# Load order, zero fills, root, softmax place and last stores of a one-core attention and GEGLU kernel

**The chip, the cores and the metric.** One core of one Trainium2 chip. Times are device microseconds (us) of one execution; the profile shows another, recorded one, with its own time. Engines in the profile: PE is TensorE's matmul side, PEld its weight load, DVE is VectorE, ACT ScalarE, POOL GpSimd; SP issues the transfers, and SPq and the like are an engine's queue.

## The reference

A layer norm without weights, a sliding dilated attention of 32 heads of width 16 (8 keys, every second position back) and a GEGLU block side by side, and the sum of both with the input:

```python
def _layernorm(x, axis=-1, eps=1e-5):
    return (x - mean) / jnp.sqrt(var + eps)          # cut: mean and var over the last axis

def _A_ref(x, wqkv, wo):                              # H = 32, Dh = 16, W = 8, dil = 2
    q, k, v = ...                                     # x @ wqkv, split by head
    kg = k[:, :, idx_c, :].reshape(B, H, S, W, Dh)    # idx = pos - 2 * arange(8)
    logits = jnp.einsum("bhsd,bhswd->bhsw", q, kg) * scale
    logits = jnp.where(mask[None, None, :, :], logits, -1e9)
    attn = _softmax(logits, axis=-1)
    o = jnp.einsum("bhsw,bhswd->bhsd", attn, vg)
    return o.reshape(B, S, D) @ wo                    # cut: a transpose

def _B_ref(x, w_gate, w_up, w_down):
    return (gelu(x @ w_gate) * (x @ w_up)) @ w_down   # Dff = 1376

xn = _layernorm(x)                                    # x: 1 x 2048 x 512, bf16
return x + _A_ref(xn, A_wqkv, A_wo) + _B_ref(xn, B_w_gate, B_w_up, B_w_down)
```

## The kernel before

The kernel states its work as tasks. Each has an engine, a name, an assumed duration, what it reads and writes, and a priority. A list scheduler in the file turns them into one fixed order per engine and sets the semaphores. So an edit of a priority can move many instructions. The parts that the change touches, in outline (some lines are shortened, and those with a bare task name stand for the whole task):

```python
SHIFT = {"acc0": 555, "acc1": 267, ...}               # cut: priority offsets by group
SCHED = dict(PE_SLACK=1.0, DMA_BPUS=250e3,
             TOL=dict(pe=1.0, act=-0.3, dve=0.3, pool=-0.3, sp=0.0))
# ... zero fills on GpSimd: the dummy matmuls' source, and a padding row block of Wd and of HT
G.task("pool", "c_wsrc", 0.8, lambda e: e.memset(wsrc[:, :], 0.0), wr=[I_wsrc], prio=PC - 1)
G.task("pool", "c_wdz", 0.3, lambda e: e.memset(Wd[0:32, 10, :], 0.0), wr=[(I_wd, 2)], prio=PC2 + 20)
G.task("pool", "c_htz", 0.3, lambda e: e.memset(HT[0:32, :, 10, :], 0.0), wr=[I_htz], prio=PC2 + 20)
# ... loads, all on one queue: Wq, Wk, Wv at -900, -899, -898; x0 in two halves at -960;
#     x1 (row tiles 2 and 3 in one load) at -899.5, so the queue has x0 x0 Wq x1 Wk
t_ld["w" + nm] = G.task("sp", "ld_w" + nm, 0, mk(), wr=[(I_wq, nm)], prio=-900 + i, nbytes=512 * 1024)
# ... layer norm of row tile t: statistics, aggregate, variance + eps, root by GpSimd's power,
#     reciprocal, subtraction, scaling; then four PE transposes
"bnst%d"  # dve bn_stats          "bnag%d"  # dve bn_aggr        "ve%d"    # dve add 1e-5
"sq%d"    # pool pow 0.5          "rstd%d"  # dve reciprocal     "sub%d"   # dve (tile 0: act)
"norm%d"  # dve scaling           "tpx.."   # pe transposes      "evx.."   # act eviction
chain(["bnst0", "bnag0", "ve0", "bnst1", "rstd0", "norm0", "bnag1", "ve1", "sub1", "rstd1", "norm1",
       "bnst2", "bnag2", "ve2", "sub2", "bnst3", "rstd2", "norm2", "bnag3", "ve3", "sub3", "rstd3",
       "norm3"])                                      # dve order of tiles 0 to 3
# ... the softmax of one block of 512 rows: logits in two PSUM banks (lgv), the rest in SBUF (DE)
"d1_%d"   # dve max over the 8 keys, from PSUM
"d2_%d"   # dve DE = logits - max
"exp%d"   # act DE = exp(DE)
"d4_%d"   # dve strided sum of DE      "d5_%d"  # dve reciprocal      "d6_%d"  # dve PB = DE * that
# ... the last matmuls (4 with Wo, 11 with Wd), the last add and the last stores
TAIL_SPLIT = [14, 15]                                 # the last two row tiles in two parts of 256
```

At the start PE first runs dummy matmuls on zeros (tile wsrc). Then it transposes the four tiles of block 0 one by one, and between them makes the q and k projections of each. The fixed order of PE is: transposes 0, q projection of tile 0, transposes 1, k of 0, q of 1, transposes 2, k of 1, transposes 3, and on.

## Time and profile before

| | before |
|---|---|
| median of 3 runs (range) | 197.95 us (197.94 to 198.12) |
| time of the profiled run, its span | 198.39 us, 196.6 us |
| PE busy | 188.7 us, 96% of the span |
| start of the last of the four transposes | 12.70 us |
| from there to the end of PE's last matmul | 181.39 us |
| from there to the last store's landing | 2.10 us |

In a timeline line the first number is the start in us from the span's start, the second the length, then engine, source line, operation, tiles, and in brackets the idle time of the engine just before it and what ended it. One more passage of the timeline belongs to those that the prediction shows; it is why the fourth tile (index 3) came late:

```profile
9.08 0.94 POOL L824 MEMSET HT<- 32x1024 bf16 x1
...
11.08 0.70 DVE L920 BATCH_NORM_STATS2 st<-XIN 128x6 f32<-128x512 bf16 x1 [0.38 <-DMA XIN<-in_A_x_dram]
...
11.91 0.13 DVE L943 RECIPROCAL rstd<-sq 128x1 f32<-128x1 bf16 x1
...
12.29 0.35 DVE L967 TENSOR_SCALAR XIN<-XIN,rstd 128x512 bf16<-128x512 bf16 x1
```

The statistics at 11.08 are those of row tile 4, which nobody needs yet. They stand in VectorE's list ahead of tile 3's reciprocal (11.91) and scaling (12.29), which PE waits for.

### The profile page before, as it was taken

How to read it: one execution, taken by the hardware profiler on the slowest of the kernel's cores; microseconds unless marked ns; L12 is line 12 of the kernel's file. 1: busy time of each engine (PE TensorE's matmuls, PEld its weight loads, DVE VectorE, ACT ScalarE, POOL GpSimd, SP SyncE). 2: the span in 40 equal slices, each digit the busy share in tenths (PEclk: the TensorE clock that was granted, in tenths of full speed). 3: DMA queues.
4: the chain of work that ended last, by engine and by line, in shares of the span. 5: the costliest groups of instructions: out<-in, count | busy, mean ns of one | idle time of the engine just before them, and what ended most of it. 6: DMA issues, size and time to landing. Idle time of an engine off the chain costs nothing.

```text
span 196.6 us, 3169 instructions
## 1 busy us (share of the span) xinstructions
PE 188.7 (96%) x1189; PEld 90.6 (46%) x1208; DVE 153.6 (78%) x238; ACT 103.6 (53%) x167; POOL 21.4 (11%) x37
## 2 busy tenths in 40 slices
PE   7689999999999999999999999999999999999994
PEld 2486444444444443444444444444444443444483
DVE  3788999999999399998999889988791897142131
ACT  4366673687787758701647930473894105766000
POOL 6834001020870100000000000000000000000000
PEclk9999999999999999999999999999999999999999
DMA  5999999894444678054538036248414260010121
GB/s 127 363 370 332 318 175 147 227 279 94 106 126 110 179 121 210 0 145 125 161 107 213 5 118 171 64 129 210 114 53 110 71 169 27 0 34 25 36 84 42
DMA packets 34639, 27.03 MB, mean 137 GB/s; under 512 B 10976, under 2 KB 33088, under 8 KB 34624
## 3 DMA queue, kind: packets, MB, share of 16 engines
q1 hardware_dynamic: 34624, 26.83, 52.9%
q8 instruction: 9, 0.15, 0.3%
q14 instruction: 6, 0.05, 0.1%
HBM read 19.99 MB, written 5.26 MB: 128 GB/s over the span
## 4 chain that ended last, share of the span: by engine, by line
PE 91%; DMA 4%; SPq 1%; DVE 1%; issue 1%; ACT 0%; DVEq 0%
PE PS L1326 35%; PE PS L1405 19%; PE PS L1084 18%; PE PS L1401 7%; PE PS L1168 4%; DMA XIN<-in_A_x_dram 4%; PE PS L1295 3%; PE PS L1040 2%; PE PS L1361 2%; PE PS L1161 1%; SPq L859 1%; SPq L905 0%; DVE st L920 0%; ACT UU L1343 0%; SPq L909 0%
## 5 line engine op out<-in xcount | busy, mean ns | idle before, releaser
L1405 PE MATMUL PS<-Wd,HT 128*128 128x512 bf16 (+1 forms) x197 | 41.3, 355 | 0.1
L1326 PE MATMUL PS<-xnT,Wu 128*128 128x512 bf16 x158 | 40.2, 379 | 0.1
L1326 PE MATMUL PS<-xnT,Wg 128*128 128x512 bf16 x153 | 39.6, 379 | 0.7 <-issue 0.3
L1274 DVE TENSOR_TENSOR UNI<-BS,PT 128x2048 bf16<-128x2048 bf16 x32 | 37.2, 1219 | 2.2 <-PE PS L1295 2.1
L1138 DVE TENSOR_TENSOR UNI<-QT,KT 128x2048 bf16<-128x2048 bf16 x32 | 37.3, 1216 | 0.9 <-ACT KT L1059 0.9
L1336 ACT ACTIVATE GG<-PS 128x512 bf16<-128x512 f32 x40 | 24.0, 600 | 23.7 <-PE PS L1326 23.7
L1084 PE MATMUL PS<-xnT,Wqkv 128*128 128x512 bf16 x157 | 35.9, 379 | 0.3 <-issue 0.2
L1343 ACT ACTIVATE UU<-PS 128x512 bf16<-128x512 f32 x40 | 23.9, 601 | 7.7 <-PE PS L1326 7.7
L1405 PEld LDWEIGHTS PS<-Wd,HT 128*128 128x128 bf16 x198 | 19.4, 98 | 18.7
L1348 DVE TENSOR_TENSOR HT<-GG,UU 128x512 bf16<-128x512 bf16 x40 | 15.8, 415 | 12.4 <-ACT UU L1343 11.8
L1326 PEld LDWEIGHTS PS<-xnT,Wg 128*128 128x128 bf16 x160 | 15.3, 98 | 19.8 <-ACT UU L1343 0.8
L1326 PEld LDWEIGHTS PS<-xnT,Wu 128*128 128x128 bf16 x160 | 15.5, 98 | 19.2 <-ACT GG L1336 0.4
L1084 PEld LDWEIGHTS PS<-xnT,Wqkv 128*128 128x128 bf16 x160 | 15.4, 98 | 18.8 <-issue 0.4
L1425 DVE TENSOR_TENSOR OB<-PS,XR 128x512 bf16<-128x512 f32 (+1 forms) x18 | 11.3, 630 | 15.5 <-PE PS L1405 15.4
L1108 ACT ACTIVATE VT<-PS 128x512 bf16<-128x512 f32 x16 | 9.5, 596 | 13.7 <-PE PS L1084 13.7
L1401 PE MATMUL PS<-Wo,OT 128*128 128x512 bf16 (+1 forms) x67 | 16.2, 354 | 0.2
L1306 ACT ACTIVATE OT<-PS 128x512 bf16<-128x512 f32 x16 | 8.7, 595 | 13.2 <-PE PS L1295 13.2
L920 DVE BATCH_NORM_STATS2 st<-XIN 128x6 f32<-128x512 bf16 x16 | 10.8, 685 | 3.8 <-DMA XIN<-in_A_x_dram 3.8
L937 POOL TENSOR_TENSOR sq<-ve,mhalf 128x2 bf16<-128x2 f32 (+1 forms) x10 | 6.6, 662 | 34.7 <-DVE ve L931 34.7
L1401 PEld LDWEIGHTS PS<-Wo,OT 128*128 128x128 bf16 x72 | 7.1, 98 | 7.0
L1124 POOL COPY KT<-KT 128x64 bf16<-128x64 bf16 x3 | 9.4, 3118 | 7.7 <-ACT KT L1101 6.0
L1094 ACT ACTIVATE QT<-PS 128x512 bf16<-128x512 f32 x12 | 7.1, 595 | 4.8 <-PE PS L1084 4.8
(62 smaller groups left out, 142.8 us busy)
## 6 DMA issues: line engine op xcount, KB each, us to landing
BS<-vt_scratch SPq DMA_DIRECT2D x64, 128.5 KB, 3.0
vt_scratch<-VT SPq DMA_DIRECT2D x16, 128.0 KB
XR<-in_A_x_dram SPq DMA_DIRECT2D x16, 128.0 KB, 2.1
XIN<-in_A_x_dram SPq DMA_DIRECT2D x7, 256.0 KB, 7.2
out_dram<-OB SPq DMA_DIRECT2D x14, 128.0 KB, 1.9
Wqkv<-in_A_wqkv_dram SPq DMA_DIRECT2D x3, 512.0 KB, 6.6
Wg<-in_B_w_gate_dram SPq DMA_DIRECT2D x1, 1280.0 KB
Wu<-in_B_w_up_dram SPq DMA_DIRECT2D x1, 1280.0 KB
```

The source lines that it names most:

```text
L920: return lambda e: e.bn_stats(out=st[:, t, :], in_=XIN[:, it.slot, t2, :])
L1084: ins = e.matmul(PS[:, 512 * it.slot:512 * it.slot + HWD], lhsT=lhsT, rhs=xnT[:, itx.slot, kt, c0:c0 + HWD], start=(kt == 0), stop=(kt == 3))
L1108: return lambda e: e.activation(out=VT[:, ito.slot, 0:HWD], in_=PS[:, 512 * it.slot:512 * it.slot + HWD], func=ACTF.Identity)
L1138: return lambda e: e.tensor_tensor(out=UNI[:, it.slot, :, :], in0=bass.AP(QT, (itq.slot * 4 + g) * 512, [[NQT * 4 * 512, 128], [0, 4], [1, ...
L1274: return lambda e: e.tensor_tensor(out=bass.AP(UNI, ito.slot * 2048, [[NUNI * 2048, 128], [512, 4], [128, 4], [1, 128]]), in0=bass.AP(BS, ...
L1326: ins = e.matmul(PS[0:M, 512 * it.slot:512 * it.slot + 512], lhsT=Wx[:, kt, j * 128:j * 128 + M], rhs=xnT[:, itx.slot, kt, :], start=(kt = ...
L1336: return lambda e: e.activation(out=GG[0:M, ito.slot, :], in_=PS[0:M, 512 * it.slot:512 * it.slot + 512], func=ACTF.Gelu_apprx_tanh)
L1343: return lambda e: e.activation(out=UU[0:M, ito.slot, :], in_=PS[0:M, 512 * it.slot:512 * it.slot + 512], func=ACTF.Identity)
L1348: return lambda e: e.tensor_tensor(out=HT[0:M, ito.slot, j, :], in0=GG[0:M, ig.slot, :], in1=UU[0:M, iu.slot, :], op=ALU.mult)
L1401: ins = e.matmul(PS[:, 512 * it.slot:512 * it.slot + CW], lhsT=OT[:, ito.slot, dq, ti * 128:(ti + 1) * 128], rhs=Wo[:, dq, c0:c1], start=( ...
L1405: ins = e.matmul(PS[:, 512 * it.slot:512 * it.slot + CW], lhsT=HT[:, ith.slot, j, ti * 128:(ti + 1) * 128], rhs=Wd[:, j, c0:c1], start=Fal ...
L1425: return lambda e: e.tensor_tensor(out=OB[:, ito.slot, 0:CW], in0=PS[:, 512 * it.slot:512 * it.slot + CW], in1=XR[:, itx.slot, c0:c1], op= ...
```

## The change

The intent: bring both weight blocks of the first projections ahead of x1, keep GpSimd out of VectorE's way, get the first two tiles' roots sooner, take a slow strided sum out of SBUF, and leave less to do after the last matmul. The core of the diff (cut: the removal of DE's helpers, the `it_pb` lines, items that are only declared, a part that is switched off; the NMS and NSUBA lines gather settings that stand one by one in the file: the N.. are numbers of buffers, NSUBA and NSQA the numbers of row tiles whose subtraction and whose root ScalarE does):

```diff
-SHIFT = {"acc0": 555, "acc1": 267, ...}
+SHIFT = {"acc0": 47, "acc1": -436, ...}               # cut: all offsets set anew
-SCHED = dict(PE_SLACK=1.0, ... TOL=dict(pe=1.0, act=-0.3, dve=0.3, ...))
+SCHED = dict(PE_SLACK=1.6, ... TOL=dict(pe=0.6, act=-0.3, dve=-0.3, ...))
-    NMS 2, NDE 1, NBS 3, NOB 2, NSUBA 1
+    NMS 1, NBS 4, NOB 3, NSUBA 0, NSQA 2
-    TAIL_SPLIT = cfg.get("TAIL_SPLIT", [14, 15])
+    TAIL_SPLIT = {14: [(0, 256), (256, 512)], 15: [(0, 256), (256, 384), (384, 512)]}
-        G.task("pool", "c_wsrc", 0.8, ... prio=PC - 1)
+        G.task("dve", "c_wsrc", 0.25, ... prio=PC - 1)
-        G.task("pool", "c_wdz", 0.3, ... prio=PC2 + 20)
-        G.task("pool", "c_htz", 0.3, ... prio=PC2 + 20)
+        G.task("dve", "c_wdz", 0.25, ... prio=PC + 1)
+        G.task("dve", "c_htz", 0.4, ... prio=PC + 2)
-            out=onef[:, 1:2], in_=onef[:, 0:1], func=ACTF.Gelu_apprx_tanh),
+            out=onef[:, 1:2], in_=onef[:, 0:1], func=ACTF.Sqrt),
-            ... prio=-900 + i, nbytes=512 * 1024)                     # Wq, Wk, Wv
+            ... prio=(-958, -957.5, -898)[i], nbytes=512 * 1024)
-                prio=(0, -899.5, -897.5, -897)[p] ...                 # x1 and later
+                prio=(0, -957, -897.5, -897)[p] ...
+                def mk_sa(t=t):
+                    return lambda e: e.activation(out=sq[:, t:t + 1], in_=mv[:, t, 1:2], func=ACTF.Sqrt,
+                                                  bias=eps[:, 0:1])
+                if t < NSQA:
+                    t_of["sq%d" % t] = G.task("act", "sq%d" % t, 0.15, mk_sa(), ...)
-        chain(["bnst0", "bnag0", "ve0", "bnst1", "rstd0", "norm0", "bnag1", "ve1", "sub1", ...
-               ... "norm3"])
+        chain(["bnst0", "bnag0", "sub0", "rstd0", "norm0", "bnst1", "bnag1", "sub1", ...
+               ... "norm3", "bnst4"])
+        chain(["norm3", "bnst5"])
+        chain(["evx0_0", "sq1"])
-                    out=dev(), in0=lgv(...), in1=msb(0), op=ALU.subtract)
+                    out=lgv(...), in0=lgv(...), in1=msb(0), op=ALU.subtract)
-                return lambda e: e.activation(out=DE[...], in_=DE[...], func=ACTF.Exp)
+                return lambda e: e.activation(out=lgv(...), in_=lgv(...), func=ACTF.Exp)
-                return lambda e: e.tensor_reduce(out=msv(1), in_=devw(), axis=AX.X, op=ALU.add)
+                return lambda e: e.tensor_reduce(
+                    out=msv(1), in_=lgv(0, 128, [(1, 128), (128, 8)]), axis=AX.X, op=ALU.add)
-                    in0=dev(), in1=msb(2), op=ALU.mult)
+                    in0=lgv(0, 128, [(512, 2), (128, 4), (1, 128)]), in1=msb(2), op=ALU.mult)
```

## The prediction

> **What bounds the kernel now.** I read the page's busy table first, then its picture of 40 slices, then the list of who waited for whom on TensorE, then the timeline of the two stretches that these leave: the first 13 us and the last 10 us.
>
> ```profile
> PE 188.7 (96%) x1189; PEld 90.6 (46%) x1208; DVE 153.6 (78%) x238; ACT 103.6 (53%) x167; POOL 21.4 (11%) x37
> ...
> PE   7689999999999999999999999999999999999994
> ```
>
> TensorE (PE) is busy 188.7 of 196.6 us, and its row dips only in the first three slices and the last one; slice four to slice 39 are full. Because a busy PE is not proof of a dense PE, I checked the spacing: in the list of the chain in order of time, 40 matmuls of 512 columns (the projection, from 44.21) take 8.63 us, 0.2157 us each, and the same 0.216 holds wherever I looked. The work itself cannot be packed more tightly, and no part of the change takes a matmul away.
>
> ```profile
> engine line waited for: us in total, times, longest us
> PE PS L1040 <- DMA Wqkv<-in_A_wqkv_dram: 1.6, 2, 0.9
> PE PS L850 <- POOL wsrc L800: 1.4, 1, 1.4
> PE PS L992 <- DVE XIN L967: 0.7, 1, 0.7
> PE PS L1326 <- issue: 0.3, 2, 0.2
> PE PS L992 <- DVE XIN L964: 0.2, 1, 0.2
> ```
>
> Every wait of PE above 0.3 us belongs to the head: two for the q and k weights (L1040), one for the zeros of the dummy matmuls (L850), two for normalized rows that it transposes (L992). After the last transpose all waits together are about 0.7 us. So the middle, some 167 us, has almost nothing to give; only head and tail do.
>
> ```profile
> 2.98 0.69 DVE L920 BATCH_NORM_STATS2 st<-XIN 128x6 f32<-128x512 bf16 x1 [2.98 <-DMA XIN<-in_A_x_dram]
> ...
> 4.16 0.57 POOL L937 TENSOR_TENSOR sq<-ve,mhalf 128x1 bf16<-128x1 f32 x1 [0.95 <-DVE ve L931]
> ...
> 6.73 1.05 PE L1040 MATMUL PS<-xnT,Wqkv 128*128 128x128 bf16 x16 [0.66 <-DMA Wqkv<-in_A_wqkv_dram]
> ...
> 7.36 0.69 DVE L920 BATCH_NORM_STATS2 st<-XIN 128x6 f32<-128x512 bf16 x1 [0.41 <-DMA XIN<-in_A_x_dram]
> ...
> 8.90 1.96 PE L1040 MATMUL PS<-xnT,Wqkv 128*128 128x128 bf16 x32 [0.90 <-DMA Wqkv<-in_A_wqkv_dram]
> ...
> 9.42 0.75 DVE L967 TENSOR_SCALAR XIN<-XIN,rstd 128x512 bf16<-128x512 bf16 x1
> ...
> 12.70 0.40 PE L992 MATMUL PS<-ident,XIN 128*128 128x128 bf16 x4 [0.72 <-DVE XIN L967]
> ```
>
> This is the head: x rows 0 and 1 land by 3.4; Wq ends the wait at 6.7; the third and fourth row tile (one load, x1) at 7.36; Wk at 8.9; the fourth tile is normalized at 12.64 and its transpose starts at 12.70. From there PE never stops, so the head is worth what moves this 12.70.
>
> **What the Trainium skill says.** "DMA: Bandwidth & Descriptors", Queues, rings and completion order: on each DMA engine the descriptors of one issuing sequencer are consumed in ring order. The trace agrees: Wq, x1, Wk land in the order of their issues, about 0.7 us for x1's 256 KB and 1.5 us for Wk's 512 KB, some 350 GB/s. So moving Wk ahead of x1 is an exchange, not a gain. "SBUF — State Buffer", SBUF: two separate sides, says VectorE in a two-port mode and GpSimd exclude each other; the trace agrees, for the scaling at 9.42 took 0.75 us beside GpSimd's memset of HT (9.08 to 10.02) and 0.35 elsewhere. "VectorE: DVE Perf Modes", the perf-mode tier table: a reduce and an fp32 tensor_tensor run at the base rate, in SBUF or PSUM. For the tensor_tensor the trace agrees, 1.22 us from PSUM and 1.21 from SBUF; for the reduce it does not quite:
>
> ```profile
> L1224 DVE TENSOR_REDUCE ms<-DE 128x128 f32<-128x1024 f32 x4 | 7.7, 1914 | 2.1 <-ACT DE L1219 2.1
> ...
> L1208 DVE TENSOR_REDUCE ms<-PS 128x128 f32<-128x1024 f32 x4 | 4.9, 1221 | 0.6 <-PE PS L1168 0.6
> ```
>
> The same strided sum costs 1.91 us from SBUF and 1.22 from PSUM. "ScalarE: Activation LUTs", What ACT_TABLE_LOAD costs: a table load is 1283 ns, as in this trace (1.28), and one more is needed, since the first table is now the root's and the GELU's is loaded later.
>
> **The change part by part.** *First loads.* The queue now has x0, x0, Wq, Wk, x1. Wq keeps its third place, so the first projection still starts near 6.7. Wk comes when 256 KB less lies ahead of it: 8.85 - 0.74, about 8.1. x1 comes where Wk came: 8.85 instead of 7.33.
>
> *Root on ScalarE, zero fills on VectorE.* For the first two tiles the variance's add (0.15) and GpSimd's power (0.57 to 0.60, with hand-overs 0.85) become one ScalarE activation of one column. The ScalarE subtraction at 3.92 took 0.72 for 512 columns; its slope leaves about 0.3 for one column. The first tile's transpose can start near 4.9 instead of 5.46. The dummy matmuls start near 1.1 instead of 1.38, as VectorE fills their source at 0.8 with nothing before it. None of this reaches the path: the next thing, the q projection, waits for Wq at 6.6 anyway. Worth 0. The two other fills leave GpSimd, so the 0.75 us scaling becomes 0.35; that does count, for it is in the chain of tile three.
>
> *The new chain to the last transpose.* VectorE's order is now fixed: all of tiles two and three before tile four, where before the statistics of tile four cut in at 11.08 and held the reciprocal to 11.91. I lay it out with start-to-start gaps from the trace. Statistics at 8.88; aggregate +0.73; add +0.21; subtract +0.07; next statistics +0.26 (10.15); reciprocal +0.61; scaling +0.18 (10.94); next aggregate +0.27; add +0.20; GpSimd power +0.24 and 0.59 long; reciprocal at 12.27; scaling 12.47 to 12.82; transpose at 12.87. The chain from landing to transpose shrinks from 5.34 to 4.0 us, the landing comes 1.52 later, and the sum is 12.87 against 12.70: **+0.17 us**. PE's earlier start on the k projection (8.1 for 8.9) ends in a longer wait before tile two's transpose, near 10.1 to 11.3.
>
> *Softmax in PSUM.* The strided sum saves 0.69 us four times on VectorE; the subtraction, exponential and scaling stay at 1.22, 1.06 and 1.21. It lies beside matmuls, so it is worth 0 directly. Its price is that a pair of the eight PSUM banks is held until the scaling, not until the subtraction. By the order of instructions, the first pair is wanted again 12 groups of matmuls after it was filled (12 x 0.863 = 10.4 us), the next two over 20 us after; the softmax of block 0, with other VectorE work between, comes to about 9 us by the durations above. Enough, with some 1.4 us of slack.
>
> *The new order in the middle.* PE does the same groups in another order. Products, exponentials and GELUs stay ahead of their matmuls when I sum durations along both orders, with 1 us or so of slack at the tightest places. I count back 0.1 of the present waits: **-0.1**.
>
> *Tail.*
>
> ```profile
> 192.81 1.25 PE L1405 MATMUL PS<-Wd,HT 128*128 128x256 bf16 x10
> ...
> 194.18 0.42 DVE L1425 TENSOR_TENSOR OB<-PS,XR 128x256 bf16<-128x256 f32 x1 [1.18 <-PE PS L1405]
> ```
>
> The last 15 matmuls of 256 columns (1.64 us in the chain) become 30 of 128. The q projection shows 48 such in 2.68 us, 0.056 each, so 30 take 1.68: +0.04. The last add goes from 0.42 to about 0.29, by the step from 0.69 at 512 columns to 0.42 at 256: -0.13. The last store is 32 KB instead of 64; the issue list gives 1.5 us for 64 KB and 1.9 for 128 KB, so perhaps -0.1, less if short rows are poor.
>
> Sum: 0.17 - 0.1 + 0.04 - 0.13 - 0.1 = -0.12 us, from 197.95 to 197.83. I predict **197.8 us**.
>
> **Rivals.** *The weight wait was the bound and is gone.* For it: the 0.9 us wait at 8.9 is the largest after the start. If tiles two and three were ready in time, PE would go from 8.1 without a stop and the head would give 0.8 to 1.0: 197.0. Against it: x1 pays for it in ring order. It would need x1 to land well before 8.85, for instance because the slow start of the transfers (97 GB/s between 3 and 4 us, by the table of stages) is not repeated.
> *PSUM becomes the bound.* A held pair makes PE wait for the scaling four times, 0.5 to 1 us each: 199 to 201. For it: VectorE is 99% busy from 20 to 64 us, so a late product or a late sum passes on. Against it: the saved 0.69 us and the bank distances above.
> *The added table load stalls PE.* 1.28 us on ScalarE near 20 us, when GELU starts: with several banks free, hidden; if not, +0.5.
> *PE stays the bound and nothing shows.* That is my case: within half a microsecond of before.
>
> **Range and chances.** Head and tail together can hardly give more than 1.2 us, and 2% is 3.96 us, half of all the time in which PE does no real work (5.5 us before the first transpose, 2.5 after the last matmul, and little else). So faster by over 2% is nearly excluded. Slower by over 2% needs a repeated PSUM stall. The range 196.8 to 198.8 holds the weight rival at one end and one or two stalls at the other. Chances: faster 0.01, within 2% 0.97, slower 0.02.
>
> **What would show it.** Right: in the timeline the projection starts near 6.7 again; tile two's statistics start near 8.9; PE's waits show VectorE's scaling before the transposes, some 1.2 and 0.3 us, in place of the second weight wait; the last transpose starts near 12.9; the reduce shows 1.22 us; no PE wait over 0.3 us after 14; the last add takes 0.29. Wrong: x1 landing before 8.3, the weights before 6.2, or a PE wait for the softmax's scaling.

## The result and the profile after

The changed kernel took 197.90 us in the median of 4 runs (197.67 to 198.14), the kernel before 198.03 in 4 runs beside it (197.94 to 198.28). The ratio is 0.9991, interval 0.9974 to 1.0009: the same. Ratios here and below are the mean time of one kernel's fast runs over that of the other's of the same rounds, so not quite the ratio of the medians that are quoted.

The page after, busy table and PE's row of the picture:

```profile
PE 190.6 (97%) x1223; PEld 91.1 (46%) x1223; DVE 153.8 (79%) x241; ACT 104.0 (53%) x169; POOL 9.6 (5%) x33
...
PE   7879999999999999999999999999999999999995
```

PE's row is full from slice four to 39 as before. GpSimd went from 21.4 to 9.6 us. PE's 190.6 against 188.7 is no added work to speak of: 15 matmuls became 30 of half the width, and no matmul records are missing (1,223 for 1,223 weight loads; before 1,189 for 1,208). The waits of PE after, all that are listed:

```profile
PE PS L1026 <- DVE XIN L1001: 1.4, 2, 1.1
PE PS L864 <- DVE wsrc L813: 1.2, 1, 1.2
PE PS L1076 <- ACT xnT L1037: 0.3, 1, 0.3
```

The two waits for weights (1.6 us) are gone in this trace, and the two waits for normalized rows have grown from 0.9 to 1.4 us (the longer one 1.1). The timeline of the head after:

```profile
6.39 1.07 PE L1076 MATMUL PS<-xnT,Wqkv 128*128 128x128 bf16 x16 [0.26 <-ACT xnT L1037]
...
7.51 1.95 PE L1076 MATMUL PS<-xnT,Wqkv 128*128 128x128 bf16 x32
...
8.13 0.69 DVE L945 BATCH_NORM_STATS2 st<-XIN 128x6 f32<-128x512 bf16 x1 [1.04 <-DMA XIN<-in_A_x_dram]
...
10.61 0.40 PE L1026 MATMUL PS<-ident,XIN 128*128 128x128 bf16 x4 [1.14 <-DVE XIN L1001]
...
12.15 0.40 PE L1026 MATMUL PS<-ident,XIN 128*128 128x128 bf16 x4 [0.26 <-DVE XIN L1001]
```

The k projection (7.51) no longer waits. VectorE waits for x1 until 8.13, and PE waits 1.14 us for tile 2. The last transpose starts at 12.15, against 12.70, and it seems that 0.55 us was won here. Most of that is not the change: the first loads are held up in the fourth microsecond, and when they land differs from run to run. The trace's table of DMA shows it for the kernel before; first the stretch from 3 to 4 us, then the one from 5 to 6:

```profile
DMA packets 98, 0.10 MB, mean 97 GB/s; under 512 B 3, under 2 KB 98, under 8 KB 98
```

```profile
DMA packets 395, 0.38 MB, mean 381 GB/s; under 512 B 23, under 2 KB 395, under 8 KB 395
```

From 3 to 4 us the queue moved a quarter of what it moved two microseconds later. In all ten traces it is slow there: 85 to 158 GB/s, after 219 to 254 in the microsecond before, and 351 to 388 from 5 to 6. The profiled run of the kernel before had drawn a poor start: it took 198.39 us, 0.36 above the median of the rounds, and its Wq, the third load in every one of these kernels, landed at 6.59, the latest of the ten traces (5.67 to 6.59). So the landing of Wq is the yardstick of a run's draw, and the table of all traces gives the last transpose less that landing too. This takes it that what stands behind Wq in the queue does not move its landing: it came at 5.95 to 6.59 with x1 behind it and at 5.67 to 6.48 with Wk, ranges that overlap; more is not shown. Landings are the last of a load's 16 parts in the trace's records.

| trace | Wq | Wk | x1 | last transpose | less Wq | last transpose to PE's end |
|---|---|---|---|---|---|---|
| before | 6.59 | 8.85 | 7.33 | 12.70 | 6.11 | 181.39 |
| after | 6.03 | 7.44 | 8.11 | 12.15 | 6.12 | 181.41 |
| x1 first again (e1) | 5.95 | 8.07 | 6.61 | 11.03 | 5.08 | 181.41 |
| VectorE's order only (e2) | 6.13 | 8.57 | 6.81 | 11.53 | 5.40 | 181.38 |
| tail undone (e3) | 6.04 | 7.43 | 8.11 | 12.15 | 6.11 | 181.37 |
| sum twice (e4) | 5.67 | 7.20 | 7.88 | 11.92 | 6.25 | 181.44 |
| load order only (e5) | 5.83 | 7.31 | 8.06 | 12.96 | 7.13 | 181.39 |
| root on GpSimd (e6) | 6.35 | 7.73 | 8.40 | 12.42 | 6.07 | 181.41 |
| x1 split (e7) | 6.20 | 8.01 | 8.36 (second half) | 11.13 | 4.93 | 181.42 |
| after, once more (e8) | 6.48 | 7.87 | 8.61 | 12.66 | 6.18 | 181.41 |

Read by that yardstick, before (6.11, one trace) and after (6.12, 6.18) have the same head within 0.07 us. And the last column is the same in ten traces to 0.07 us: in both orders of the middle, once PE has its last transpose, it needs 181.4 us.

Two further groups after, from the list by line and shape (busy us and mean ns after the bar), are the strided sum and the GELU's table loads:

```profile
L1367 ACT ACT_TABLE_LOAD x5 | 6.4, 1283 | 0.1
...
L1254 DVE TENSOR_REDUCE ms<-PS 128x128 f32<-128x1024 f32 x4 | 4.9, 1225 | 1.7 <-ACT PS L1249 1.4
```

The sum now takes 1,225 ns for 1,914, and there are five GELU loads for four. The end of the timeline after:

```profile
193.65 0.29 DVE L1456 TENSOR_TENSOR OB<-PS,XR 128x128 bf16<-128x128 f32 x1 [0.55 <-PE PS L1436]
```

The last add takes 0.29 us for 0.42. From PE's end to the last store's landing it is 1.88 us (193.56 to 195.44), against 2.10 before (194.09 to 196.19).

### The profile page after: what moved, and what is told of

Same layout as the page of the kernel before. It is cut to its first block, busy times and chain, and to the rows that moved or that the text cites. A ratio compares the mean times of both kernels' runs of the same rounds, so it can differ in the third digit from the quotient of the medians.

```text
span 196.0 us, 3243 instructions
## 1 busy us (share of the span) xinstructions
PE 190.6 (97%) x1223; PEld 91.1 (46%) x1223; DVE 153.8 (79%) x241; ACT 104.0 (53%) x169; POOL 9.6 (5%) x33
## 4 chain that ended last, share of the span: by engine, by line
PE 93%; DMA 3%; DVE 2%; SPq 1%; issue 0%; POOL 0%; DVEq 0%
PE PS L1357 36%; PE PS L1436 19%; PE PS L1120 18%; PE PS L1432 7%; PE PS L1326 4%; PE PS L1204 4%; DMA XIN<-in_A_x_dram 3%; PE PS L1076 2%; PE PS L1392 2%; PE PS L1197 1%; DVE st L945 1%; SPq L881 0%; SPq L929 0%; DVE XIN L1001 0%; POOL sq L969 0%
## 5 line engine op out<-in xcount | busy, mean ns | idle before, releaser
L1436 PE MATMUL PS<-Wd,HT 128*128 128x512 bf16 (+2 forms) x209 | 41.3, 345 | 0.0
L1357 PE MATMUL PS<-xnT,Wg 128*128 128x512 bf16 x160 | 40.3, 379 | 0.0
L1374 ACT ACTIVATE UU<-PS 128x512 bf16<-128x512 f32 x40 | 24.0, 600 | 10.5 <-PE PS L1357 10.4
L1456 DVE TENSOR_TENSOR OB<-PS,XR 128x512 bf16<-128x512 f32 (+2 forms) x19 | 11.5, 605 | 17.7 <-PE PS L1436 17.7
L1432 PE MATMUL PS<-Wo,OT 128*128 128x512 bf16 (+2 forms) x76 | 16.9, 345 | 0.0
L1137 ACT ACTIVATE KT<-PS 128x512 bf16<-128x512 f32 x12 | 7.2, 597 | 4.8 <-PE PS L1120 4.8
L969 POOL TENSOR_TENSOR sq<-ve,mhalf 128x2 bf16<-128x2 f32 (+1 forms) x8 | 5.5, 686 | 64.3 <-DVE ve L956 64.3
```

The source lines that it names most:

```text
L1357: ins = e.matmul(PS[0:M, 512 * it.slot:512 * it.slot + 512], lhsT=Wx[:, kt, j * 128:j * 128 + M], rhs=xnT[:, itx.slot, kt, :], start=(kt = ...
L1374: return lambda e: e.activation(out=UU[0:M, ito.slot, :], in_=PS[0:M, 512 * it.slot:512 * it.slot + 512], func=ACTF.Identity)
L1432: ins = e.matmul(PS[:, 512 * it.slot:512 * it.slot + CW], lhsT=OT[:, ito.slot, dq, ti * 128:(ti + 1) * 128], rhs=Wo[:, dq, c0:c1], start=( ...
L1436: ins = e.matmul(PS[:, 512 * it.slot:512 * it.slot + CW], lhsT=HT[:, ith.slot, j, ti * 128:(ti + 1) * 128], rhs=Wd[:, j, c0:c1], start=Fal ...
L1456: return lambda e: e.tensor_tensor(out=OB[:, ito.slot, 0:CW], in0=PS[:, 512 * it.slot:512 * it.slot + CW], in1=XR[:, itx.slot, c0:c1], op= ...
```

## The experiments

Two theories stood against each other. Mine: the load order is an exchange in one ring; it takes from the third and fourth tile what it gives to Wk, the new VectorE order pays that back, and nothing else of the change but the tail reaches the end. The rivals: the wait for Wk was the bound, so the load order by itself gains; and the pair of PSUM banks held longer, or the retuned middle, moves time that something else hides. Edits of an order below are made after scheduling: the named tasks swap places in one engine's list, and all else stays. The one exception is e7, where the load had to be split before scheduling: there a later x load also moved one place, ahead of a load of Wo.

**e1: x1 ahead of Wk again, in the changed kernel.**

```diff
+        # SP's list: x0 x0 Wq Wk x1  ->  x0 x0 Wq x1 Wk
+        _reorder(G, "sp", ["ld_x1", "ld_wk"])
```

> The changed kernel with one thing undone: the second x load stands again ahead of the k weights on the queue (x, x, Wq, x, Wk); no other instruction moves. Theory (the new load order is an exchange, and the fixed VectorE order is what shortens the chain): x1 lands where the k weights landed in the changed kernel less half, near 6.7 to 6.8, the k weights near 8.1; k projection from 8.1, tile three ready near 10.8, so PE runs on from 8.1 and the last transpose starts near 11.4 instead of 12.15: about 0.7 us less, 197.2. Rival (the weight wait was the bound, the new order of loads is the gain): the last transpose is later than 12.15 and the time is 198.3 or more. Second rival (what the head saves is lost again later): last transpose earlier, time 197.9.

Measured: 196.58 us (196.42 to 197.62, 6 runs), ratio to before 0.9940 (0.9917 to 0.9963). In the same rounds the changed kernel with its tail undone had 0.9988 and with the sum doubled 0.9992, so undoing this one exchange gains about 0.5%, 1.0 us, where I had expected 0.7. The timeline of the head:

```profile
7.01 0.69 DVE L981 BATCH_NORM_STATS2 st<-XIN 128x6 f32<-128x512 bf16 x1
...
8.12 1.96 PE L1112 MATMUL PS<-xnT,Wqkv 128*128 128x128 bf16 x32 [0.33 <-DMA Wqkv<-in_A_wqkv_dram]
...
11.03 0.39 PE L1062 MATMUL PS<-ident,XIN 128*128 128x128 bf16 x4
```

Tile 2's statistics start at 7.01 with no wait. PE waits 0.33 us for Wk at 8.12, and from there it runs without a stop: the last transpose has no bracket, so it came when PE was ready, not when the rows were. A wait for weights that is still there costs less than the wait for rows that took its place.

**e2: VectorE's order alone, in the kernel before.**

```diff
+        # DVE's list: tile 3's reciprocal and scaling ahead of tile 4's statistics
+        _reorder(G, "dve", ["rstd3", "norm3", "bnst4", "bnag4", "sub4"])
```

> The kernel before with one part of the change alone: VectorE finishes tile three (reciprocal, scaling) ahead of the statistics of tile four; five instructions of one engine change places, nothing else. Theory: tile three is ready near 11.7 instead of 12.64, and PE, which ends the projection before it near 12.0, takes the last transpose at once: 12.0 for 12.70, so 0.7 us less, 197.3. Rival (the landing of x1 or the weights set the end of the head, not VectorE's order): no change, 198.0.

Measured: 197.08 us (196.87 to 197.36, 6 runs), ratio 0.9956 (0.9935 to 0.9977), 0.9 us faster, where I had expected 0.7; by the yardstick it is 0.71 (5.40 for 6.11). The timeline:

```profile
8.61 1.96 PE L1076 MATMUL PS<-xnT,Wqkv 128*128 128x128 bf16 x32 [0.63 <-DMA Wqkv<-in_A_wqkv_dram]
...
8.93 0.75 DVE L1003 TENSOR_SCALAR XIN<-XIN,rstd 128x512 bf16<-128x512 bf16 x1
...
11.53 0.39 PE L1028 MATMUL PS<-ident,XIN 128*128 128x128 bf16 x4
```

Again the last transpose follows PE's own work. The scaling at 8.93 still takes 0.75 us beside GpSimd's fill of HT, as before, and it does not matter here: PE is at the k projection until 10.4 anyway. So a reorder of five small VectorE instructions, one part of the change, is worth most of a microsecond alone.

**e3: the tail undone, in the changed kernel.**

```diff
-    TAIL_SPLIT = {14: [(0, 256), (256, 512)], 15: [(0, 256), (256, 384), (384, 512)]}
+    TAIL_SPLIT = {14: [(0, 256), (256, 512)], 15: [(0, 256), (256, 512)]}
```

> The changed kernel with its last tile in two stores of 256 columns as before, not three. Theory: the last add 0.42 instead of 0.29 us, the last store 64 KB instead of 32, the last matmuls 0.04 us less in sum: 0.1 to 0.25 us more, 198.0 to 198.15. Rival (short matmuls and short rows cost more than they save): 0.1 to 0.3 less.

Measured: 197.75 us (197.57 to 197.81, 5 runs), ratio 0.9988 (0.9968 to 1.0007). The loss that I expected is not to be seen in the times: e4, which has the small stores, took 197.77 in the same rounds. The trace shows it. The last add of e3:

```profile
193.61 0.42 DVE L1456 TENSOR_TENSOR OB<-PS,XR 128x256 bf16<-128x256 f32 x1 [1.18 <-PE PS L1436]
```

It is 0.42 us again, and from PE's end to the last landing it is 2.11 us (193.52 to 195.63), against 1.88 (after), 1.87 (e4) and 1.87 (e8). PE in return is 0.04 us shorter (181.37 for 181.41). Net 0.19 us by the traces, which is below what 5 runs with a scatter of 0.2 to 0.6 us can resolve.

**e4: the strided sum twice in each block, in the changed kernel.** The result is right; the two sums of a softmax start 1.14 us apart, so VectorE has about 1.1 us more in each and holds the two PSUM banks that much longer.

```diff
+                    e.tensor_reduce(out=msv(2), in_=lgv(0, 128, [(1, 128), (128, 8)]), axis=AX.X, op=ALU.add)
                     return e.tensor_reduce(
                         out=msv(1), in_=lgv(0, 128, [(1, 128), (128, 8)]), axis=AX.X, op=ALU.add)
```

> The changed kernel with the strided sum of the softmax done twice in each of the four blocks (the first result is overwritten): VectorE works 4 x 1.22 us more, and each pair of PSUM banks is held that much longer; the order of all else is the same. Theory (sum and banks lie beside the matmuls): no change within 0.3 us, 197.9, busy VectorE 158.7, and no wait of PE above 0.3 us after 14. Rival (VectorE or the held banks are near the bound, so the 0.69 us saved by the sum in PSUM was worth something): 0.5 to 4.9 us more, 198.4 to 202.8, with PE waiting for the scaling or for the products.

Measured: 197.77 us (197.46 to 198.09, 6 runs), ratio 0.9992 (0.9972 to 1.0012). The busy table:

```profile
PE 188.7 (96%) x1204; PEld 91.0 (46%) x1223; DVE 157.9 (81%) x245; ACT 103.9 (53%) x169; POOL 9.6 (5%) x33
```

VectorE has four instructions and 4.1 us more (157.9 for 153.8; I had expected 158.7, but the two sums overlap a little), and PE from the last transpose on 181.44 us for 181.41. More than was saved by moving the sum (four times 0.69 us) can be put back without effect. This rules out both a gain from the softmax in PSUM and a stall by its banks.

**e5: the load order alone, in the kernel before.**

```diff
+        # SP's list: x0 x0 Wq x1 Wk  ->  x0 x0 Wq Wk x1
+        _reorder(G, "sp", ["ld_wk", "ld_x1"])
```

> The kernel before with the new load order alone (x, x, Wq, Wk, x): two transfers change places, nothing else. Theory (an exchange that the old VectorE order pays for): the weights come near 7.5 to 8.1 and the wait for them shrinks, x1 lands near 8.1 to 8.8, the old chain of 5 us follows, the last transpose starts near 13.2: 0.4 to 0.8 us more, 198.4 to 198.8. Rival (the wait for the k weights was the bound): 0.7 us less, 197.2.

Measured: 198.93 us (198.52 to 199.51, 6 runs), ratio 1.0043 (1.0029 to 1.0058): 0.8 to 0.9 us slower, where I had expected 0.4 to 0.8; by the yardstick it is 1.02 (7.13 for 6.11). The timeline:

```profile
8.01 1.95 PE L1076 MATMUL PS<-xnT,Wqkv 128*128 128x128 bf16 x32
8.09 0.69 DVE L956 BATCH_NORM_STATS2 st<-XIN 128x6 f32<-128x512 bf16 x1 [1.14 <-DMA XIN<-in_A_x_dram]
...
10.14 0.75 DVE L1003 TENSOR_SCALAR XIN<-XIN,rstd 128x512 bf16<-128x512 bf16 x1
...
10.95 0.40 PE L1028 MATMUL PS<-ident,XIN 128*128 128x128 bf16 x4 [0.99 <-DVE XIN L1003]
...
11.35 0.69 DVE L956 BATCH_NORM_STATS2 st<-XIN 128x6 f32<-128x512 bf16 x1
...
12.96 0.40 PE L1028 MATMUL PS<-ident,XIN 128*128 128x128 bf16 x4 [0.71 <-DVE XIN L1003]
```

The wait for Wk is gone here too (8.01, no bracket), and the kernel is slower. This is what refutes the rival of the weight wait. From the start of tile 2's statistics to the last transpose it is 4.87 us (8.09 to 12.96), against 4.02 in the changed kernel (8.13 to 12.15). The 0.85 us are the scaling beside GpSimd's fill (0.75 for 0.35) and tile 4's statistics at 11.35, which again stand ahead of tile 3's last steps.

**e6: the root of tiles 0 and 1 back on GpSimd, in the changed kernel** (without the 1e-5). The outputs are right.

```diff
-   sq0, sq1 on ACT:  e.activation(out=sq[:, t:t + 1], in_=mv[:, t, 1:2], func=ACTF.Sqrt, bias=eps[:, 0:1])
+   sq0, sq1 on POOL: e.tensor_tensor(out=sq[:, t:t + 1], in0=mv[:, t, 1:2], in1=mhalf[:, 0:1], op=ALU.pow)
```

> The changed kernel with the root of the first two tiles back on GpSimd's power (without the 1e-5, which their variance of 0.16 does not feel); all other instructions keep their order. Theory (tiles zero and one lie off the path, since PE waits for tile two anyway): the first projection starts 0.2 to 0.4 us later, the last transpose still near 12.1, the time is that of the changed kernel within 0.3, 197.9. Rival (the faster root is what the head gained): 0.3 to 0.6 more, 198.2 to 198.5.

Measured: 197.74 us (197.45 to 198.10, 6 runs), ratio 0.9984 (0.9972 to 0.9996); the changed kernel itself in the same rounds has 0.9983 (e8). The timeline:

```profile
6.63 1.07 PE L1112 MATMUL PS<-xnT,Wqkv 128*128 128x128 bf16 x16 [0.36 <-ACT xnT L1073]
...
8.42 0.69 DVE L981 BATCH_NORM_STATS2 st<-XIN 128x6 f32<-128x512 bf16 x1 [1.09 <-DMA XIN<-in_A_x_dram]
...
12.42 0.40 PE L1062 MATMUL PS<-ident,XIN 128*128 128x128 bf16 x4 [0.24 <-DVE XIN L1037]
```

The first projection starts 0.24 us later than after's 6.39, and the last transpose comes 4.00 us after tile 2's statistics, as in the changed kernel. The root on ScalarE is worth nothing here.

**e7: x1 in two halves, Wk between them, in the changed kernel.** A try at a better version: tile 2 needs only the first half.

```diff
-   x0 x0 Wq Wk x1
+   x0 x0 Wq x1a Wk x1b        # x1a: row tile 2, x1b: row tile 3, 128 KB each
```

> A version meant to beat both: the changed kernel with the second x load in two halves, one ahead of the k weights and one behind (x, x, Wq, half x, Wk, half x). Theory: tile two lands near 6.3, the k weights near 7.75 (0.35 earlier than with all of x1 ahead), tile three near 8.1 and ready 2.5 us after, near 10.6; PE goes from 7.8, the last transpose starts near 10.7 instead of 11.03: 0.3 us less than with x1 whole and ahead (196.6), 196.3. Rival (tile three becomes the bound, or smaller loads land no sooner): 196.6 to 197.2.

Measured: 196.70 us (196.63 to 196.99, 5 runs), ratio 0.9933 (0.9921 to 0.9945). The 196.3 that I expected was not reached; the time lies in the rival's range. The timeline:

```profile
8.06 1.96 PE L1114 MATMUL PS<-xnT,Wqkv 128*128 128x128 bf16 x32 [0.38 <-DMA Wqkv<-in_A_wqkv_dram]
...
8.38 0.69 DVE L983 BATCH_NORM_STATS2 st<-XIN 128x6 f32<-128x512 bf16 x1
...
11.13 0.40 PE L1064 MATMUL PS<-ident,XIN 128*128 128x128 bf16 x4
```

Wk lands 1.81 us after Wq instead of 2.12 in e1. By the yardstick the last transpose is 0.15 us better (4.93 for 5.08). Tile 3's statistics now start at 8.38, 2.75 us before its transpose, so the rows are nearly late again. The two ratios overlap and come from different rounds: which of e1 and e7 is faster stays open. Both beat the kernel before by about 0.6%, and the changed kernel too.

**e8: the changed kernel once more, beside e5 to e7.** No edit.

> The changed kernel itself once more, in the same rounds as the three others. Both theories: 197.7 to 198.0. Its trace shows how much the landing of the first loads moves from run to run: Wq at 6.0 within 0.4 us.

Measured: 197.71 us (197.55 to 198.18, 6 runs), ratio 0.9983 (0.9971 to 0.9996). The profiled run was a slow draw, 198.18 us, and its Wq landed at 6.48, just outside the expected 0.4 us around 6.0. Its timeline:

```profile
6.61 1.05 PE L1076 MATMUL PS<-xnT,Wqkv 128*128 128x128 bf16 x16 [1.13 <-DMA Wqkv<-in_A_wqkv_dram]
...
8.64 0.69 DVE L945 BATCH_NORM_STATS2 st<-XIN 128x6 f32<-128x512 bf16 x1 [1.97 <-DMA XIN<-in_A_x_dram]
...
12.66 0.40 PE L1026 MATMUL PS<-ident,XIN 128*128 128x128 bf16 x4 [0.26 <-DVE XIN L1001]
```

The last transpose is 0.51 us later than in the first trace of the same kernel (12.66 for 12.15), and the run is 0.51 us longer (198.18 for 197.67). Of that, 0.45 is the landing of Wq. So a scatter of half a microsecond in this kernel's head is the draw of its first transfers, and single traces of the head must not be compared without it.

One more thing is seen here alone, for this is the same kernel as after. Its busy table and its waits have

```profile
PE 188.5 (96%) x1204; PEld 90.9 (46%) x1223; DVE 153.9 (78%) x241; ACT 104.1 (53%) x169; POOL 9.6 (5%) x33
```

```profile
PE PS L1357 <- issue: 0.8, 5, 0.2
```

where the trace after has 1,223 matmuls and no such wait, with the same 181.41 us of PE. Here 19 matmul records are missing, one of them in each gap after the last transpose: from one matmul's start to the next recorded one it is 0.54 us there, with two weight loads between, where the trace after has 0.31 and 0.23. The trace before lacks 19 records too, and its waits on "issue" are of the same kind.

## Why the prediction held, point by point

The median fell within 0.1 us of the predicted 197.8, but two small terms of its sum were off, in opposite directions: +0.17 for the head and -0.1 for the middle, and neither was there. That they nearly cancel is luck.

- **What bounds the kernel.** PE from the last transpose on: shown by the 181.37 to 181.44 us of ten traces, in which the order of the middle, the softmax's place, four more sums and three load orders differ. The start of the last transpose and the tail are all that moves the time.
- **The head, predicted +0.17: about 0 measured.** The mechanism was right on both sides. x1 behind Wk shifts tile 2's start, and the new VectorE order with the fills out of the way shortens the chain from there; e5 and e2 show the two alone, +0.85 and -0.87 us by their ratios, +1.02 and -0.71 by the yardstick (e2 without the fills). The chain's new length was right: 4.02 us from the statistics to the last transpose, in the after trace and in e8 (8.64 to 12.66), where the laid-out steps gave 3.99. What was mis-sized is the later landing of x1. I took 1.52 us, the distance from x1 to Wk in the trace before. Behind Wq, x1 landed 0.74 us later before, and 2.08 and 2.13 later in the two traces after: a shift of 1.34 to 1.39. With 5.34 less 4.02, 1.32 us, given back by the chain, 0.02 to 0.07 us remain. The absolute times of the prediction (projection 6.7, landing 8.85, last transpose 12.87) are all too late against the first trace by 0.3 to 0.7 us because they were read from a trace with a poor draw; against e8 they are 0.1 to 0.24 off. Two of my own signs of error did appear in the first trace: x1 landed before 8.3 (8.11), and Wq before 6.2 (6.03). In e8 neither did (8.61 and 6.48). Of the 0.74 us by which x1 was early in the first trace, 0.56 are the draw, for Wq was earlier by as much, and the rest is the mis-sized shift.
- **PE's waits.** Predicted: some 1.2 and 0.3 us for rows in place of the second weight wait, and none over 0.3 after 14 us. Measured: 1.14 and 0.26, and none.
- **Root, fills, table load: predicted 0, measured 0.** The first transpose came at 5.06 (predicted 4.9) and the dummies at 1.25 (predicted 1.1). That the root has no effect is shown by e6; the fill of the dummies' source was not run alone. The fifth GELU table load, 1.28 us, shows in no wait of PE. The HT fill is the exception that the prediction had named: 0.40 us in tile 2's chain, visible in e5, absent after.
- **Softmax: predicted 0 directly, measured 0.** The sum takes 1,225 ns as predicted; e4 shows that neither the saving nor the longer hold of two banks reaches the end. In the trace after, block 0 takes 8.7 us from the mask to the end of the scaling (32.38 to 41.09), where I had estimated 9 (and VectorE from 20 to 64 us before was busy 98%, not 99).
- **The middle, predicted -0.1: 0 measured.** From the last transpose to PE's end it is 181.41 for 181.39 us, of which 0.04 is the narrower last matmuls. The small waits of PE that the prediction hoped to win back were no waits at all but holes in the record, as e8 shows, so there was nothing to count back (its "about 0.7 us" after the last transpose is 0.8 in the list, five times 0.16; and its "some 167 us" of middle are 181.4). That the new offsets gain nothing in the middle is shown by this sum; they were not run alone.
- **The tail, predicted +0.04 - 0.13 - 0.1: measured +0.04 and -0.23.** The three steps hold in the traces of e3 against after, e4 and e8. It is the only part of the change whose gain is kept, 0.19 us, and the medians cannot resolve it; the ratios 0.9991 and 0.9983 of the changed kernel (-0.18 and -0.34 us) are in line with it.

Of the rivals, the weight wait as the bound is refuted by e5 and e1, the PSUM stall by e4, and the table load by PE's list of waits. "PE stays the bound and nothing shows" is what happened, but it hides a gain of 0.9 us and a loss of 0.85 us inside one change. What makes the first transfers' packets slow, and why that varies, is open.

## What to carry to other kernels

When one queue brings everything, an earlier load is paid for by a later one, and the question is which consumer has the longest chain behind its landing: here the rows (4.0 us of VectorE, GpSimd and PE steps to the last transpose), not the weights, which are used at once. A change made of several parts that comes out "the same" is worth taking apart, for it may hold a gain and its loss; here undoing one exchange of two loads gave 1.0 us. And before comparing heads of two traces, line them up on a transfer that stands in the same place in both.

## What the Trainium skill lacked or had wrong

- "TensorE: Matmul & The Clock Gate", Back-to-back issue gap: it gives about 81 ns per matmul of 128 columns and about 131 ns of 512 for a stream with weight loads, and calls 56 and 216 ns the gap of an isolated matmul. In this kernel, where every matmul has its own weight load, 40 matmuls of 512 columns took 8.63 us (216 ns each) and 48 of 128 columns 2.68 us (56 ns each). The figures called isolated are the ones that hold here, and the section "Wait — 56ns, not 53.3ns?" of the same page gives 55.6 and 215.7 ns for matmuls back to back.
- No page has the dip in a program's first transfers: 85 to 158 GB/s in the fourth microsecond against 351 to 388 in the sixth, and the third load landing anywhere from 5.67 to 6.59 us in ten traces. Two profiled runs of the same kernel differ by 0.51 us (197.67 and 198.18), and 0.45 of that is this landing.
- "VectorE: DVE Perf Modes", the perf-mode tier table: a reduce has one rate in it, wherever its operand lies. The same strided fp32 sum of 128x1024 took 1,914 ns from SBUF and 1,225 ns from PSUM here. The page "SBUF — State Buffer" (Door 1: The DMA port swizzle, a note on "cachelines") says that an access in SBUF that crosses to a new line of 16 bytes pays a penalty, but not how much. That the stride is the reason here is not shown, for no run has such a sum in SBUF without a stride.
